# Who zeroes the third value buffer, and the order of turns, logits and divisions, in a fused attention and mixture-of-experts kernel

## The chip, the cores and the metric

The kernel runs on one core of a Trainium2 chip. The metric is the device time of one execution in microseconds (us). The kernel before takes 343.18 us, the median of three runs between 341.76 and 344.17. The engines are named as the profile names them: PE multiplies matrices and turns (transposes) tiles, DVE is the vector engine, ACT the scalar engine, POOL the GpSimd engine, which here also issues most loads, and SP issues the other transfers. Each engine works through its own list of instructions in order and waits where one needs a result that is not there yet.

## The reference

First an attention over chunks of 32 positions (4 batches, 8 heads, 768 positions, head dimension 64). Each chunk sees 16 positions before it, 8 behind it and 8 memory positions:

```python
scores = scale * np.matmul(q_c, k_full.transpose(0, 1, 3, 2))
scores = scores - np.max(scores, axis=-1, keepdims=True)
a = np.exp(scores)
a = a / (np.sum(a, axis=-1, keepdims=True) + 1e-09)
out[:, :, c_start:c_end] = np.matmul(a, v_full)
```

Its result, 3072 rows of 512, goes to a router with 8 experts. Each row takes the two experts with the highest noisy logits:

```python
logits = x @ w_gate
noise_scale = np.log1p(np.exp(x @ w_noise))
noisy_logits = logits + noise_scale * noise
top2 = np.argpartition(-noisy_logits, 2, axis=1)[:, :2]
...
h = np.maximum(x[mask] @ w1[e], 0.0)
out[mask] += top2_w[mask, k, None] * (h @ w2[e])
```

## The kernel before, in words

**Units.** The attention runs in 16 units, numbered i = 0 to 15 here. One unit is half of the positions of a group of four heads; there are eight groups, and a group has two units, an even one and the odd one behind it. A batch is four units. Queries and keys are loaded by group and must be turned before they can be used; one turn (`qkT_pe(n)`, line 243) handles a pair of heads, and a group has two pairs, so there is one turn per unit. The scores of both units of a group need both of its pairs.

**What one unit does.** On PE the probabilities of the unit before are turned (`PT_pe`, line 312), then queries and keys of a later pair (`qkT_pe`, line 250), then come the value products of the unit before (`PV_pe`, lines 326 and 330), the scores of the next unit (`scores_pe`, lines 275 to 290), and the turn of a finished output (`xT_pe`, line 354). DVE takes the maximum of the scores (line 298), copies the turned probabilities (line 317), subtracts the maximum (line 303), and divides the unit before by its sums (`mult_dve`, lines 342 and 343). ACT copies the turned queries (line 253), takes the exponential (line 305), copies the turned keys in two halves (`kT_act`, line 261) and copies the turned output (line 356). The order on each engine is the order in which the loop of line 576 calls these steps; it is written out by hand (`manual_schedule`), and no planner moves anything.

**Buffers.** Scores have one buffer (two PSUM banks), value products have one (three banks), and everything that is turned, the logits and the small products of the router share three (`psT`). A PE instruction that needs a buffer waits until its last reader is done. Turned queries and keys have four buffers each, so turns can run ahead: `ahead(i)` says which pairs unit i turns. Up to unit 4 that is pair i + 2, in unit 5 pairs 7 and 8, and from unit 6 on pair i + 3.

**Values.** Value tiles lie in three buffers, used by the eight groups in the order 0, 1, 0, 2, 1, 0, 2, 1. The places that no load writes must be zero, so each buffer is zeroed once before its first load: `clear_v` on ACT, `zero_v` (line 136) on DVE or POOL, and two direct fills on POOL (lines 570 and 571). A buffer has 24 chunks of 512 bf16 elements per partition; `zero_v` fills six of them. DVE's fills are issued as 32-bit words, POOL's as bf16. Buffer 1 has one fill on DVE in unit 0, and buffer 2 has three on DVE in units 2, 3 and 4 and one on POOL in unit 3. The loads themselves (lines 112 and 120) are issued by POOL.

**Routing inside the attention.** When four units of a batch b are finished, `begin_route(b)` computes the logits (line 365, PE), their exponential, logarithm and a copy (lines 380 to 384, ACT), and the noisy logits and their differences (lines 392 to 407, POOL for batches 0 to 2). It runs in units 6, 10 and 14. The rest follows in stages, one per unit: selection (lines 399 to 424 on DVE, the pair table of line 430 and its products, lines 472 and 473, on POOL), ranks (lines 437 to 442 on PE, 448 to 460 on DVE), comparison with a ramp (line 465, DVE) and the table of rows (line 480, PE; 486 or 488, DVE). `early_steps` runs the PE part of a stage ahead of the value products, `late_steps` the rest. The fourth batch is routed after the last unit, in one go, on DVE.

**The end.** Finished rows go to DRAM (`write_rows`, SP). After the fourth batch's table, POOL gathers rows per expert pair by indirect transfers (line 682) and the experts run: `first` (line 746) and `second` (line 754), with their weights loaded by POOL (lines 523 and 528).

These lines of the loop are the ones that move:

```python
            if fresh:
                begin_route((i - 3) // HP)
...
            if i < NPAIR - 1:
                late_steps()
            if i in (2, 3, 4):
                zero_v(2, i - 2)
            if i >= 1:
                mult_dve(i - 1)
```

Of the kernel before, what the change touches and what calls it, by code (L numbers as in the profile page):

```python
# [20 lines left out]
I32 = mybir.dt.int32  # L21
# [3 lines left out]
def kernel(  # L25
# [14 lines left out]
    nc = tc.nc  # L40
# [12 lines left out]
    HP = H // 2  # L53
# [31 lines left out]
    def body():  # L85
# [16 lines left out]
        def new_group(g):  # L102
            qg = ap_.tile([128, 2 * GP, SJ * D], BF16, name="qg", bufs=3)
            kg = ap_.tile([128, 2 * GP, SJ * D], BF16, name="kg", bufs=3)
            groups[g] = (qg, kg, vbufs[turn_of[g]])
# [25 lines left out]
        def zero_k(x):  # L131
            for hh in range(2):
                nc.vector.memset(kbufs[x][64 * hh:64 * hh + 64, 1 - hh, :], 0.0)

        def zero_v(x, j, eng=None):
            (eng or nc.vector).memset(vbufs[x][:, 6 * j:6 * j + 6], 0.0)  # L136

        new_group(0)
        load_qk(0, 0)
        identb = const.tile([128, 128], BF16, name="identb")  # L140
# [113 lines left out]
                else:  # L254
                    st[n]["p_k"] = p_t

        def kT_act(n):
            st[n]["kT"] = kbufs[n % NKB]
            for hh in range(2):
                hs = slice(64 * hh, 64 * hh + 64)  # L260
                nc.scalar.copy(st[n]["kT"][hs, hh, :].rearrange("d (p j) -> d p j", j=SJ), st[n]["p_k"][hs].rearrange("d j p -> d p j"))  # L261

# [38 lines left out]
        def sub_dve(n):  # L301
            sd = ap_.tile([128, 2, BT, CTX], F32, name="sd")
            nc.vector.tensor_tensor(out=sd, in0=st[n]["ps"], in1=bc4(st[n]["mx"], CTX), op=Alu.subtract)  # L303
            P = ap_.tile([128, 2 * UB, 4, QW], BF16, name="P")
            nc.scalar.activation(out=P.rearrange("p x h c -> p h x c"), in_=sd.rearrange("p x (h u) (e c) -> p (x h) (u e) c", h=2, e=2), func=Act.Exp, scale=scale)  # L305
            st[n]["P"] = P
# [8 lines left out]
        def PT_dve(n):  # L315
            PT = ap_.tile([128, 2 * UB, 128], BF16, name="PT")
            nc.vector.tensor_copy(PT, st[n]["p_p"])  # L317
            st[n]["PT"] = PT
# [219 lines left out]
        def begin_route(b):  # L538
            logits_pe(b)
            begin, *rest = route(b)  # L540
            begin()
            while pending:
                early_steps()
                late_steps()
            pending.extend(rest)
            for x in ((1,), (2, 3))[b] if b < 2 else ():
                load_noise(x)
# [19 lines left out]
        new_group(2)  # L567
        load_qk(2)
        memory_values(0, 2)
        nc.gpsimd.memset(vbufs[1][:, 12:15], 0.0)  # L570
        nc.gpsimd.memset(vbufs[1][:, 21:24], 0.0)
        def ahead(i):
            return [i + 2] if i < NEAR else [n for n in (i + 2, i + 3) if n < NPAIR and (i == NEAR or n > i + 2)]

        NEAR = 5
        for i in range(NPAIR):
            if i >= 1:
                PT_pe(i - 1)
            max_dve(i)
            for n in ahead(i):  # L580
                qkT_pe(n)
            fresh = i >= 3 and (i - 3) % HP == HP - 1
            if fresh:
                begin_route((i - 3) // HP)
            early_steps()
            if i >= 1:
                PT_dve(i - 1)
            sub_dve(i)
            if i == 0:
                zero_v(1, 1)  # L590
                load_v(1)
                new_group(3)
                load_qk(3)
            if i == 1:
                zero_k(3)
            for n in ahead(i):
                kT_act(n)
            if i >= 1:
                PV_pe(i - 1)
            if i + 1 < NPAIR:  # L600
                scores_pe(i + 1)
            if i < NPAIR - 1:
                late_steps()
            if i in (2, 3, 4):
                zero_v(2, i - 2)
            if i >= 1:
                mult_dve(i - 1)
                if i - 1 == NPAIR - 2:
                    write_rows(B, B - 1, 0, UB, 0, XC)
            if i >= 2:  # L610
                xT_pe(i - 2)
            if i == 2:
                load_v(2)
                memory_values(2, NG)
            for n in ahead(i):
                g = n // GP + 3
                if n % GP == 1 and g < NG:
                    new_group(g)
                    load_qk(g)
            if i == 3:  # L620
                zero_v(2, 3, nc.gpsimd)
                ramps()
                load_router()
            if i == 4:
                load_v(3)
            if i == 5:
                constants()
            if i >= 4 and i % GP == 0 and i // GP + 2 < NG:
                load_v(i // GP + 2)
            if i == GP * (NG - 3) + 1:  # L630
                load_w1(0)
                load_w2(0)
                load_w1(1)
        n = NPAIR - 1
        PT_pe(n)
        PT_dve(n)
        xT_pe(n - 1)
        late_steps()
        PV_pe(n)
        mult_dve(n)  # L640
        write_rows(B + 1, B - 1, UB, BT, 0, XC)
        early_steps()
        xT_pe(n)
        late_steps()
# [323 lines left out]
```

## Time and profile before

| what | value |
|---|---|
| runs | 341.76, 343.18, 344.17 us |
| profiled execution | 340.9 us, span 339.2 us |
| mean granted clock of PE over the span | 0.968 |
| PE busy | 295.1 us (87%) |
| DVE busy | 170.8 us (50%) |
| ACT busy | 132.5 us (39%) |
| POOL busy | 137.9 us (41%) |
| maximum of the first unit starts | at 14.6 us |
| maximum of the last unit starts | at 88.6 us |
| first expert product (line 746) starts | at 112.9 us |

The busy time of an engine is an average over stages with different limits: up to about 97 us the attention, then the last routing, then the experts. The share alone therefore does not say what sets the time. A row of the timeline gives start, length, engine, line, operation, what it writes and reads, the shapes, and in brackets the idle time of the engine before it and what ended that. A row of the chain gives start, length and what. Times count from the start of the span.

### The profile page before, as it was taken

To read this page: it belongs to the slowest core of one execution; us is meant where nothing else is said; L and a number is where in the kernel's file an instruction comes from. 1 tells how busy PE (TensorE), PEld (TensorE's weight loads), DVE (VectorE), ACT (ScalarE), POOL (GpSimd) and SP (SyncE) were. 2 spreads that over 40 slices of the span, in tenths; PEclk is the share of its full clock that TensorE was granted. 3 is DMA by queue.
4 is the path that set the end of the run, shared out by engine and by line. 5 is a ranking of instruction groups with operands and counts; after the bars stand their busy time and mean duration, and the time that the engine had idled before them with its cause. 6 is when DMAs were issued, how large, how long until landed. Compare 5 with 4: busy or idle time off the path is not lost.

```text
span 339.2 us, 8160 instructions
## 1 busy us (share of the span) xinstructions
PE 295.1 (87%) x3492; PEld 180.0 (53%) x3492; DVE 170.8 (50%) x341; ACT 132.5 (39%) x232; POOL 137.9 (41%) x181
## 2 busy tenths in 40 slices
PE   1687888898753859999999999999999999999990
PEld 1566676776542645548547545545545545545540
DVE  7788779889686653224224233224413424434430
ACT  7867888795430423343333323223123113103100
POOL 8878885392233686400062043034250132141161
PEclk9999999999985699999999999999999999999997
DMA  7999999999991379970059129518849227221031
GB/s 102 183 180 192 187 164 198 221 104 164 228 276 26 96 111 226 224 130 2 2 84 229 31 60 198 95 56 148 181 107 200 57 80 126 40 93 53 6 130 66
DMA packets 58407, 42.87 MB, mean 126 GB/s; under 512 B 32215, under 2 KB 51799, under 8 KB 58368
## 3 DMA queue, kind: packets, MB, share of 16 engines
q0 software_dynamic: 49808, 38.80, 68.9%
q1 hardware_dynamic: 8272, 3.44, 4.7%
q8 instruction: 29, 0.48, 0.5%
q10 hardware_dynamic: 288, 0.07, 0.1%
q14 instruction: 10, 0.08, 0.1%
HBM read 61.32 MB, written 10.65 MB: 212 GB/s over the span
## 4 chain that ended last, share of the span: by engine, by line
PE 54%; issue 16%; DVE 15%; ACT 6%; POOL 5%; DMA 1%; POOLq 0%; DVEq 0%
PE ps_h L746 23%; PE ps_y L754 19%; POOL out_dram L762 4%; ACT kd L261 3%; DVE vg L136 2%; DVE mx L298 2%; DVE sd L303 2%; PE p_t L691 2%; DVE xrow L343 2%; PE ps_o L330 2%; PE ps_o L326 2%; ACT xt L356 2%; ACT P L305 1%; ACT qT L253 1%; PE ps_s L285 1%
## 5 line engine op out<-in xcount | busy, mean ns | idle before, releaser
L746 PE MATMUL ps_h<-xTb,w1t 128*128 128x512 bf16 (+3 forms) x608 | 106.6, 325 | 2.0 <-DVE xTb L692 2.0
L754 PE MATMUL ps_y<-w2t,ht 128*128 128x512 bf16 x448 | 102.0, 379 | 0.0
L746 PEld LDWEIGHTS <-w1t 128*128 128x128 bf16 x864 | 64.1, 97 | 45.2 <-DVE xTb L692 1.6
L762 POOL DMA_INDIRECT out_dram<-acc,sidx x28 | 27.9, 995 | 139.2 <-DVE acc L761 135.0
L734 DVE TENSOR_SCALAR ht<-ps_h 128x416 bf16<-128x416 f32 (+2 forms) x64 | 39.9, 625 | 72.8 <-PE ps_h L746 72.8
L732 ACT ACTIVATE ht<-ps_h 128x416 bf16<-128x416 f32 (+2 forms) x72 | 37.9, 526 | 76.7 <-PE ps_h L746 72.4
L754 PEld LDWEIGHTS <-ht 128*128 128x128 bf16 x448 | 41.9, 98 | 46.6
L758 ACT ACTIVATE acc<-ps_y,meta 128x512 f32<-128x512 f32 x28 | 19.2, 687 | 69.3 <-PE ps_y L754 56.5
L746 PE MATMUL ps_h<-xTs,w1t 128*128 128x32 bf16 x256 | 45.4, 177 | 0.2 <-DVE xTs L707 0.2
L761 DVE SCALAR_TENSOR_TENSOR acc<-ps_y,meta,acc 128x512 f32<-128x512 f32 x28 | 21.0, 751 | 37.0 <-PE ps_y L754 37.0
L682 POOL DMA_INDIRECT xl<-x_rows,gidx x28 | 29.7, 1061 | 15.4 <-issue 6.1
L120 POOL DMA_DIRECT2D vg<-in_v_dram x34 | 25.3, 753 | 8.2 <-PE ps_s L290 3.4
L692 DVE COPY xTb<-p_t 128x512 bf16<-128x512 bf16 x28 | 11.7, 422 | 29.0 <-PE p_t L691 29.0
L261 ACT COPY kd<-p_t 64x768 bf16<-64x768 bf16 x32 | 25.2, 786 | 1.0 <-PE p_t L250 0.7
L250 PE MATMUL p_t<-identb,qg 128*64 128x128 bf16 x192 | 10.3, 245 | 8.2 <-DMA qg<-in_q_dram 6.3
L305 ACT ACTIVATE P<-sd 128x768 bf16<-128x768 f32 x16 | 13.5, 844 | 9.5 <-DVE sd L303 9.5
L356 ACT COPY xt<-p_x 128x768 bf16<-128x768 bf16 x16 | 12.8, 798 | 8.0 <-PE p_x L354 7.7
L343 DVE TENSOR_TENSOR xrow<-ps_o,rec 128x768 bf16<-128x768 f32 x16 | 15.3, 958 | 0.6
L326 PE MATMUL ps_o<-memv,PT 128*128 128x260 bf16 x96 | 13.7, 279 | 2.0 <-DVE PT L317 2.0
L298 DVE TENSOR_REDUCE mx<-ps_s 128x12 f32<-128x768 f32 x16 | 15.1, 941 | 0.6 <-PE ps_s L285 0.6
L303 DVE TENSOR_TENSOR sd<-ps_s,mx 128x768 f32<-128x768 f32 x16 | 15.2, 947 | 0.0
L253 ACT COPY qT<-p_t 128x768 bf16<-128x768 bf16 x16 | 12.8, 800 | 5.0 <-PE p_t L250 4.7
(146 smaller groups left out, 305.6 us busy)
## 6 DMA issues: line engine op xcount, KB each, us to landing
w1t<-in_moe_w_dram POOLq DMA_DIRECT2D x8, 1024.0 KB
w2t<-in_moe_w_dram POOLq DMA_DIRECT2D x8, 1024.0 KB
vg<-in_v_dram POOLq DMA_DIRECT2D x30, 168.0 KB
qg<-in_q_dram POOLq DMA_DIRECT2D x7, 384.0 KB
kg<-in_k_dram POOLq DMA_DIRECT2D x7, 384.0 KB
x_rows<-xrow SPq DMA_DIRECT2D x3, 792.0 KB
x_rows<-xrow SPq DMA_DIRECT2D x2, 384.0 KB
xl<-x_rows,gidx POOLq DMA_INDIRECT x28
```

Source lines behind the costliest of these rows:

```text
L120: nc.gpsimd.dma_start(out=vg[p0 + j:p0 + j + nj, c:c + n, hd, :, :].rearrange("p c e d -> p c (e d)"), in_=bass.AP(v.tensor, v.offset + (g ...
L261: nc.scalar.copy(st[n]["kT"][hs, hh, :].rearrange("d (p j) -> d p j", j=SJ), st[n]["p_k"][hs].rearrange("d j p -> d p j"))
L298: nc.vector.tensor_reduce(out=mx, in_=st[n]["ps"], axis=AX, op=Alu.max)
L303: nc.vector.tensor_tensor(out=sd, in0=st[n]["ps"], in1=bc4(st[n]["mx"], CTX), op=Alu.subtract)
L343: nc.vector.tensor_tensor(out=xr.rearrange("p u (h d) -> p u h d", d=D), in0=po[:, :, :MD].rearrange("p u (h d) -> p u h d", d=D), in1=rec ...
L682: nc.gpsimd.indirect_dma_start(out=xl, out_offset=None, in_=xd, in_offset=bass.IndirectOffsetOnAxis(ap=gidx[:, p:p + 1], axis=0), bounds_c ...
L732: nc.scalar.activation(out=dst, in_=src, func=Act.Relu)
L734: nc.vector.tensor_scalar(out=dst, in0=src, scalar1=0.0, scalar2=None, op0=Alu.max)
L746: nc.tensor.matmul(out=ps_h[:, o:o + w], lhsT=w1t[:, kp, f * 128:(f + 1) * 128], rhs=rhs(kp), start=(kp == 0 and i == 0), stop=(kp == KP - ...
L754: nc.tensor.matmul(out=ps_y, lhsT=ht[:, f, j * CAP:(j + 1) * CAP], rhs=w2t[:, f, :], start=(f == 0), stop=(f == FB - 1))
L761: nc.vector.scalar_tensor_tensor(out=a, in0=ps_y, scalar=gate, in1=a, op0=Alu.mult, op1=Alu.add)
L762: nc.gpsimd.indirect_dma_start(out=out_part[p], out_offset=bass.IndirectOffsetOnAxis(ap=sidx[:, p:p + 1], axis=0), in_=a, in_offset=None, ...
```

## The change

1. A new helper `wipe_v` zeroes a stretch of a value buffer on POOL, seen as 32-bit integers. It takes over the two fills of buffer 1 that POOL had as bf16, the fill of buffer 1 that DVE had in unit 0, and all of buffer 2: chunks 0 to 11 in unit 1 and 12 to 23 in unit 3. DVE keeps the fills of buffer 0 and one of buffer 1 before the loop.
2. `ahead(i)` is pair i + 2 in every unit that has one.
3. From unit 1 on, the first half of the turned keys is copied by ACT ahead of the unit's exponential, the second half behind it.
4. `begin_route` stands behind the scores of the next unit, ahead of the late steps; before, it stood behind the turn.
5. In the last unit the late steps (the selection of batch 2) stand behind the subtraction; before, they came after the loop. The division of unit 14 and the write of its rows move from the last unit to behind the copy of the last turned probabilities, and the turn of output 14 moves behind the last value products.

```diff
+        def wipe_v(x, lo, hi):
+            nc.gpsimd.memset(vbufs[x][:, lo:hi].bitcast(I32), 0)
...
-        def kT_act(n):
+        def kT_act(n, which=(0, 1)):
             st[n]["kT"] = kbufs[n % NKB]
-            for hh in range(2):
+            for hh in which:
...
-        nc.gpsimd.memset(vbufs[1][:, 12:15], 0.0)
-        nc.gpsimd.memset(vbufs[1][:, 21:24], 0.0)
+        wipe_v(1, 12, 15)
+        wipe_v(1, 21, 24)
+        wipe_v(1, 6, 12)
         def ahead(i):
-            return [i + 2] if i < NEAR else [n for n in (i + 2, i + 3) if n < NPAIR and (i == NEAR or n > i + 2)]
-
-        NEAR = 5
+            return [i + 2] if i + 2 < NPAIR else []
+
         for i in range(NPAIR):
...
             fresh = i >= 3 and (i - 3) % HP == HP - 1
-            if fresh:
-                begin_route((i - 3) // HP)
             early_steps()
             if i >= 1:
                 PT_dve(i - 1)
+            if i >= 1:
+                for n in ahead(i):
+                    kT_act(n, (0,))
             sub_dve(i)
             if i == 0:
-                zero_v(1, 1)
                 load_v(1)
...
+            if i == NPAIR - 1:
+                late_steps()
             for n in ahead(i):
-                kT_act(n)
+                kT_act(n, (1,) if i >= 1 else (0, 1))
             if i >= 1:
                 PV_pe(i - 1)
             if i + 1 < NPAIR:
                 scores_pe(i + 1)
+            if fresh:
+                begin_route((i - 3) // HP)
             if i < NPAIR - 1:
                 late_steps()
-            if i in (2, 3, 4):
-                zero_v(2, i - 2)
-            if i >= 1:
+            if 1 <= i < NPAIR - 1:
                 mult_dve(i - 1)
-                if i - 1 == NPAIR - 2:
-                    write_rows(B, B - 1, 0, UB, 0, XC)
             if i >= 2:
                 xT_pe(i - 2)
+            if i == 1:
+                wipe_v(2, 0, 12)
...
             if i == 3:
-                zero_v(2, 3, nc.gpsimd)
+                wipe_v(2, 12, 24)
...
         n = NPAIR - 1
         PT_pe(n)
         PT_dve(n)
-        xT_pe(n - 1)
-        late_steps()
+        mult_dve(n - 1)
+        write_rows(B, B - 1, 0, UB, 0, XC)
         PV_pe(n)
         mult_dve(n)
         write_rows(B + 1, B - 1, UB, BT, 0, XC)
+        xT_pe(n - 1)
         early_steps()
         xT_pe(n)
         late_steps()
```

## The prediction

> **What bounds the kernel now.** The profiled execution took 340.9 us, of which the span is 339.2 us; the median of the three runs shown is 343.18 us, 2.3 us more. I make the sum against the profiled execution and carry the difference over to the median unchanged.
>
> I read first the page's chain that ended last, its shares by line.
>
> ```profile
> PE ps_h L746 23%; PE ps_y L754 19%; POOL out_dram L762 4%; ACT kd L261 3%; DVE vg L136 2%; DVE mx L298 2%; DVE sd L303 2%; PE p_t L691 2%; DVE xrow L343 2%; PE ps_o L330 2%; PE ps_o L326 2%; ACT xt L356 2%; ACT P L305 1%; ACT qT L253 1%; PE ps_s L285 1%
> ```
>
> The expert stage (lines 746 and 754) holds 42% of the span, and the diff does not touch it: it can only start earlier or later. Everything else is decided in the sixteen attention units and in the routing behind the last of them, where the chain is passed between DVE, ACT and PE. The question is what one unit costs. Here is the chain through unit 13, which has no fill and no turn in it (start, length, what).
>
> ```profile
> 79.80 0.87 DVE mx L298
> 80.67 0.47 DVE PT L317
> 81.19 0.84 PE ps_o L326 x6
> 82.03 0.78 PE ps_o L330 x24
> ```
>
> Maximum, copy of the turned probabilities, then the value products end at 82.81, 3.0 us after the maximum began. On DVE the reciprocal and the division follow, and the next maximum is queued behind them.
>
> ```profile
> 34.74 0.95 DVE L303 TENSOR_TENSOR sd<-ps_s,mx 128x768 f32<-128x768 f32 x1
> 35.96 1.34 DVE L136 MEMSET vg<- 128x1536 uint32 x1 [0.27 <-issue]
> 37.21 0.17 DVE L342 RECIPROCAL rec<-ps_o 128x12 f32<-128x12 f32 x1
> 37.42 0.96 DVE L343 TENSOR_TENSOR xrow<-ps_o,rec 128x768 bf16<-128x768 f32 x1
> 38.29 0.95 DVE L298 TENSOR_REDUCE mx<-ps_s 128x12 f32<-128x768 f32 x1
> ...
> 43.19 0.23 DVE L342 RECIPROCAL rec<-ps_o 128x12 f32<-128x12 f32 x1 [2.63 <-PE ps_o L330]
> 43.46 0.96 DVE L343 TENSOR_TENSOR xrow<-ps_o,rec 128x768 bf16<-128x768 f32 x1
> 44.34 0.44 DVE L224 CAST ramp<-ramp_i 128x128 bf16<-128x128 int32 x1
> ```
>
> From reciprocal to the next DVE operation it is 44.34 - 43.19 = 1.15 us. So a unit cannot be shorter than 3.0 + 1.15 + about 0.1 of hand-over, **4.3 us**. Whatever DVE does between the subtraction and the end of the value products (some 0.9 us) is free; what goes beyond it is paid. The reader sees both in these rows. Unit 4's maximum began at 34.74 - 0.47 - 0.87 = 33.40, so it took 4.89 us with the fill of line 136 in it; unit 5 (38.29 to the maximum behind 44.34 and three small casts, 44.76) took 6.47, and its reciprocal waited 2.63 us for PE.
>
> Why PE was late is in PE's and ACT's own timelines.
>
> ```profile
> 32.83 0.25 PE L285 MATMUL ps_s<-kd,qT 128*32 128x80 bf16 x4 [1.18 <-ACT kd L261]
> ...
> 41.05 0.53 PE L250 MATMUL p_t<-identb,kg 128*64 128x128 bf16 x12 [0.89 <-ACT qT L253]
> ```
>
> ```profile
> 27.93 0.80 ACT L356 COPY xt<-p_x 128x768 bf16<-128x768 bf16 x1
> 29.27 0.80 ACT L253 COPY qT<-p_t 128x768 bf16<-128x768 bf16 x1 [0.54 <-PE p_t L250]
> 30.45 0.84 ACT L305 ACTIVATE P<-sd 128x768 bf16<-128x768 f32 x1 [0.39 <-DVE sd L303]
> 31.20 1.58 ACT L261 COPY kd<-p_t 64x768 bf16<-64x768 bf16 x2
> ```
>
> In an odd unit the scores of the next group need the key that the same unit turns (two ahead); unit 3's waited 1.18 us for it. Unit 5 turns two pairs, and the second one's key transposes waited 0.89 us for a buffer.
>
> **The change part by part.** *Fills.* Three fills of 1.34 us leave DVE in units 2 to 4 and one in unit 0. How much of each stood beyond the free 0.9 us: in unit 4 the reciprocal began at 37.21 where the value products, a quarter of a us late behind the turn, would have let it go at 33.40 + 3.4 = 36.8, so 0.4; in unit 2, whose turn is not late, about 0.55; in unit 3 nothing, since the key decides. In unit 0 no quoted row tells where the next scores end, so between nothing and 1.34; I take 0.35, near the other units. What DVE drops, POOL takes.
>
> ```profile
> L136 DVE MEMSET vg<- x8: 1338/1338/1338, 2.3 to 36.0; 128x1536 uint32 x8
> ...
> L570 POOL MEMSET vg<- x1: 1377/1377/1377, 14.7 to 14.7; 128x1536 bf16 x1
> L571 POOL MEMSET vg<- x1: 1377/1377/1377, 16.0 to 16.0; 128x1536 bf16 x1
> L136 POOL MEMSET vg<- x1: 2657/2657/2657, 34.7 to 34.7; 128x3072 bf16 x1
> ```
>
> POOL pays by the element: 1377 ns for 1536, 2657 for 3072. No row shows it filling many 4-byte words. If a word costs what a bf16 element costs, twelve chunks (3072 words) take 2.66 us, the two small fills fall to 0.74, and POOL has 2 x 2.66 + 1.38 + 2 x 0.74 - (2.66 + 2 x 1.38) = 2.8 us more. If time goes by bytes, it is 2.8 + 7.7 = 10.5 us. I take the first, since DVE's own 1536 words take 1338 ns, nearly POOL's time for as many elements. POOL issues the loads, but group 3's buffer is not read before unit 7, so I charge nothing; without that cover it would be up to the 2.8. The last query and key loads are issued a unit later too, behind a value load, and are read only in unit 12. The Trainium skill, VectorE: DVE Perf Modes, section Zero memsets can be issued as uint32 (trn2), states one cycle per element whatever the dtype; it speaks of VectorE, no run here shows it for POOL, and by it the sum would be the same 2.8 us.
>
> *Half of the key ahead of the exponential.* ACT's four operations, 0.80 + 0.80 + 1.58 + 0.84, are 4.0 us. In unit 3 it idled 0.54 and 0.39; the first half (0.79) goes where the 0.39 was, so the second half ends about 0.45 us earlier. The exponential slips by 0.4, hidden: its reader comes a unit later. With an even unit ahead, whose ACT is done early, I reckon 4.5 us for an odd unit (scores end, 0.5 to the copy, 3.6 of ACT, 0.5 of scores); unit 3 itself gains 0.5. Units 0 to 4 together: 0.35 + 0.55 + 0.5 + 0.4, **-1.8**.
>
> *One turn in unit 5.* 6.47 becomes 4.3 plus 0.42 of casts, which the key's 4.5 does not exceed: 4.75, **-1.7**. The price comes back in odd units, whose key is no longer a unit ahead: unit 13, 4.3 before, becomes 4.5, **+0.2**; unit 9 has the six comparisons of the ranks on DVE and units 7 and 11 the selection, which are as long by themselves.
>
> *Logits behind scores.* They stand ahead of the value products in units 6 and 10 (chain):
>
> ```profile
> 46.42 0.74 PE ps_l L365 x24
> ...
> 66.63 0.69 PE ps_l L365 x24
> ```
>
> Both leave the path: **-1.4**. What is late next: in units 7 and 11 the turn of the probabilities stands behind the logits on PE and ends some 1.1 us after the maximum began, by my count, where DVE would take it at 0.87: 0.2 us each, **+0.4**. The noise loads that the step issues on SP have nothing behind them that waits. And the batch's selection is late against its unit, on POOL:
>
> ```profile
> 70.69 3.62 POOL L120 DMA_DIRECT2D vg<-in_v_dram  x5 [0.28 <-issue]
> 74.32 0.52 POOL L430 TENSOR_TENSOR oh<-two 128x192 bf16<-128x192 bf16 x1
> ```
>
> ```profile
> 76.48 0.25 PE L437 MATMUL ps_r<-oh,upper 128*128 128x168 bf16 x1 [0.18 <-ACT qT L253]
> ```
>
> The pair table (line 430) is queued behind five load issues, 3.62 us, and ends at 74.84, 1.64 us before PE wants it in unit 12. The logits of batch one move behind 0.84 + 0.78 us of value products and some 0.8 of scores, less 0.4 by which these start earlier: 2.0 us later in their unit. Units 10 and 11 together are 0.5 us shorter. 2.5 against 1.64 and a hand-over: PE waits about **+1.0** at the head of its queue, with unit 12's value products and the next scores behind it.
>
> *The end.* DVE's last units:
>
> ```profile
> 92.46 0.23 DVE L342 RECIPROCAL rec<-ps_o 128x12 f32<-128x12 f32 x1 [0.88 <-PE ps_o L330]
> ...
> 94.07 0.19 DVE L399 TENSOR_REDUCE m<-nl 128x6 f32<-128x48 f32 x1
> ...
> 95.90 0.23 DVE L342 RECIPROCAL rec<-ps_o 128x12 f32<-128x12 f32 x1
> ```
>
> The selection of batch two (94.07 to 95.8, 1.73 us) lay in the shadow of the last value products. Moved ahead of unit 14's division it fills an idle 0.88 us and pushes the rest: the last value products need the one output buffer that this division frees. 1.73 - 0.88 = **+0.85**. SP's row writes move with the divisions, far ahead of the first gather.
>
> Sum: -1.8 - 1.7 - 1.4 + 0.2 + 0.4 + 1.0 + 0.85 = -2.45, **-2.5**. The profiled execution would take 338.4, the median 343.18 - 2.5 = **340.7**.
>
> **The rivals.** *One, faster:* the two new waits don't come, since POOL gets its load issued in time or the last products start anyway. For it: both are small differences of long queues. Against: the buffer and queue orders are fixed. -2.5 - 1.0 - 0.85 = -4.35: 338.8.
>
> *Two, slower:* the turn's wait comes back in full in odd units 5, 7, 9, 11 and 13. Place: PE's scores behind the key's second half. It decides where the turn's query copy ends after the subtraction; then the half put ahead only delays. For it: the 0.54 us that ACT waited for PE. Unit 3's maximum stands in the chain at
>
> ```profile
> 28.23 0.86 DVE mx L298
> ```
>
> so that unit took 33.40 - 28.23 = 5.2; less 4.3 it is 0.9 each, 4.5 for five, in place of the 0.6 already charged: -2.5 + 3.9 = +1.4, 344.6. Against: in unit 3 the query copy ended (29.27 + 0.80) before the subtraction let ACT go on.
>
> *Three:* the clock.
>
> ```profile
> 112.00:116.00 4.00, 3.48 (x19) 2.37 (x17) 3.55 (x5) 1.12 (x3) 3.29 (x3) 0.50 0.36 100
> 116.00:120.00 4.00, 2.73 (x35) 2.14 (x32) 2.91 (x13) 2.12 (x8) 2.16 (x3) 1.00 0.24 68
> ```
>
> The granted clock (third column from the end) is 0.50 as the experts begin and 1.00 from 116 us. If the return does not move with the stage, 2.5 us more run at half speed, +1.25: 341.9. The Trainium skill, TensorE: Matmul & The Clock Gate, section What's actually happening, has the clock granted by free-running windows of 3413 ns, by which the return could stay where it is; one profile cannot show whether it does.
>
> *Four, not what it says:* POOL's words go by bytes. The 7.7 us then stand ahead of the issues of groups 2 to 4, and no quoted row tells what these have in hand, so between nothing and 7.7; I take 3, near one such issue (3.62 us): +0.5, 343.7. For it: no row of POOL excludes it; against: DVE's rate.
>
> **How the numbers follow.** One per cent is about what a measurement of this kernel can tell from no change. Chances: my forecast 0.34, rival one 0.27, two 0.14, three 0.08, four 0.07, two of the last three together 0.10 (two and four 347.6). The range leaves out that last case and a little of the first: 338.2 (rival one with units 7 and 11 free too) to 345.0. Faster by over 1% (under 339.75): rival one and 0.03 of the forecast, 0.30; slower by over 1% (over 346.6): 0.10; within: 0.60.
>
> **What would show it.** Fills: no line 136 on DVE behind unit 0, POOL's at 0.74, 1.38 and 2.66. Turns: unit 5 near 4.75, PE's waits for the key under 0.8 in odd units. Logits: behind the scores in units 6 and 10, and a PE wait for the pair table in unit 12. End: unit 14's division right behind the selection, last value products waiting for it. I am wrong if odd units take over 5 us, if a load of values stops PE in units 5 to 9, or if the wait in unit 12 is missing.

## The result, and the profile after

The changed kernel takes **342.15 us** (median of 20 runs, 339.6 to 346.5), the kernel before 341.69 us (median of 20 runs, the three shown at first among them). The ratio after to before is **1.0002, 95% interval 0.9977 to 1.0027**: no change that can be measured. I had said 2.5 us less, 0.73%, which the interval excludes. The time itself lies inside the range that I gave (338.2 to 345.0); that is luck, as the account below shows. Ratios and fits here and below use the fast runs, those that nothing disturbed; the medians are of all runs. The profiled execution took 341.32 us, its span 339.6 us, 0.4 us more than the one before.

The sixteen maxima of DVE cut the attention into units, as in the prediction. The rows of the maximum's line, of the kernel before (first) and of the changed kernel (line numbers are 3 higher in the loop, 6 in the expert part):

```profile
L298 DVE TENSOR_REDUCE mx<-ps_s x16: 895/947/958, 14.6 to 88.6; 128x12 f32<-128x768 f32 x16
```

```profile
L301 DVE TENSOR_REDUCE mx<-ps_s x16: 895/948/959, 14.6 to 89.0; 128x12 f32<-128x768 f32 x16
```

Both begin at 14.6 us and their last maxima are 0.4 us apart (88.62 and 89.01). Between them lies this (unit lengths in us, each the difference of two starts of the timeline; e2, e8 and e10 are experiments below):

| unit | 0 | 1 | 2 | 3 | 4 | 5 | 6 | 7 | 8 | 9 | 10 | 11 | 12 | 13 | 14 | to index table |
|---|---|---|---|---|---|---|---|---|---|---|---|---|---|---|---|---|
| before | 3.41 | 5.21 | 4.89 | 5.26 | 4.89 | 6.47 | 5.08 | 4.97 | 4.75 | 4.47 | 5.96 | 4.98 | 4.75 | 4.30 | 4.60 | 18.04 |
| after | 3.07 | 5.44 | 4.39 | 5.16 | 4.56 | 4.84 | 4.57 | 5.55 | 6.09 | 4.68 | 5.60 | 5.55 | 5.71 | 4.66 | 4.51 | 18.60 |
| e2 | 3.07 | 6.16 | 4.30 | 4.60 | 4.57 | 4.78 | 4.38 | 5.13 | 5.36 | 4.65 | 5.89 | 5.83 | 5.44 | 4.66 | 4.51 | 18.02 |
| e8 | 3.07 | 6.10 | 4.31 | 5.32 | 4.57 | 4.68 | 4.49 | 5.39 | 6.08 | 4.66 | 5.19 | 5.14 | 5.25 | 4.84 | 4.52 | 19.27 |
| e10 | 3.07 | 5.21 | 4.31 | 4.60 | 4.57 | 4.78 | 5.49 | 4.98 | 4.87 | 4.70 | 6.65 | 4.99 | 5.16 | 4.66 | 4.66 | 17.34 |

The changed kernel is 3.2 us ahead when unit 7 begins and 0.1 us behind when unit 13 begins; the end costs 0.6 more. So in these two executions 3.2 us are gained up to unit 7 and given back in units 7 to 12. Where PE was late there, its own timeline says (changed kernel; in brackets the idle time ahead and what ended it):

```profile
24.24 0.53 PE L253 MATMUL p_t<-identb,kg 128*64 128x128 bf16 x12 [0.49 <-DMA kg<-in_k_dram]
28.60 0.38 PE L253 MATMUL p_t<-identb,qg 128*64 128x128 bf16 x7 [0.46 <-issue]
...
41.46 0.20 PE L288 MATMUL ps_s<-kd,qT 128*32 128x80 bf16 x1 [0.88 <-issue]
46.56 0.75 PE L368 MATMUL ps_l<-wgn,xt 128*128 128x16 bf16 x24 [0.36 <-ACT kd L264]
...
51.63 0.25 PE L288 MATMUL ps_s<-kd,qT 128*32 128x80 bf16 x4 [0.47 <-ACT kd L264]
53.11 0.33 PE L357 MATMUL p_x<-identb,xrow 128*128 128x128 bf16 x3 [0.67 <-issue]
...
66.09 0.49 PE L329 MATMUL ps_o<-memv,PT 128*128 128x260 bf16 x3 [0.24 <-issue]
...
72.08 0.85 PE L333 MATMUL ps_o<-vg,PT 128*32 128x256 bf16 x24 [0.61 <-DMA vg<-in_v_dram]
76.68 0.23 PE L440 MATMUL ps_r<-oh,upper 128*128 128x168 bf16 x1 [1.14 <-POOL oh L433]
...
95.30 0.84 PE L329 MATMUL ps_o<-memv,PT 128*128 128x260 bf16 x6 [1.78 <-DVE xrow L346]
```

Two of these I had forecast: the pair table in unit 12 (1.14 us) and the last value products behind unit 14's division (1.78 us). Three kinds I had not: loads that land late (unit 2's key, unit 11's value), logits and keys that delay each other at 46.56 and 51.63, and "issue", idle time with no releaser in the profile: PE stops in the middle of a run of equal instructions, for 0.24 to 0.88 us.

POOL's fills, as whole rows of the groups:

```profile
L139 POOL MEMSET vg<- 128x3072 int32 x2 | 5.4, 2678 | 0.0
...
L139 POOL MEMSET vg<- 128x768 int32 x2 | 1.4, 737 | 0.1
L139 POOL MEMSET vg<- 128x1536 int32 x1 | 1.4, 1377 | 0.0
```

A 32-bit word costs POOL what a bf16 element cost it before (1377 ns for 1536, 2657 for 3072).

### The profile page after: what moved, and what is told of

The parts are those of the page before. It is cut to its first block, busy times and chain, and to the rows that moved or that the text cites. A ratio compares the mean times of both kernels' runs of the same rounds, so it can differ in the third digit from the quotient of the medians.

```text
span 339.6 us, 8160 instructions
## 1 busy us (share of the span) xinstructions
PE 294.8 (87%) x3492; PEld 179.7 (53%) x3492; DVE 167.0 (49%) x337; ACT 132.1 (39%) x232; POOL 141.0 (42%) x183
## 4 chain that ended last, share of the span: by engine, by line
PE 70%; DMA 7%; ACT 7%; DVE 6%; POOL 4%; issue 4%; POOLq 0%; DVEq 0%; ACTq 0%
PE ps_h L752 31%; PE ps_y L760 26%; DMA kg<-in_k_dram 4%; ACT kd L264 2%; PE ps_o L329 2%; PE ps_o L333 2%; ACT xt L359 2%; DMA wgn_f<-in_moe_w_noise_dram 2%; PE p_t L697 2%; POOL out_dram L768 1%; PE ps_s L288 1%; PE p_x L357 1%; PE ps_s L779 1%; ACT P L308 1%; ACT qT L256 1%
```

## The experiments

Ratios are to the kernel before, timed on the same chip in the same session. The last column of the table compares at equal clock: each run lists the mean granted clock of PE, and a straight line through the runs of a session, with one slope for all its kernels, rises by 0.9 to 1.4 us for every 0.005 that the clock is lower. The column gives the distance from the kernel before along that line (with its 95% uncertainty). It is not a time: where a kernel itself lowers its clock, the column leaves that loss out.

| kernel | median, us | before, us | ratio, 95% interval | at equal clock, us |
|---|---|---|---|---|
| e1 logits back | 342.61 | 341.84 | 1.0007 (0.9979 to 1.0036) | +0.2 ± 0.7 |
| e2 end back | 341.03 | 341.84 | 0.9989 (0.9961 to 1.0018) | -0.5 ± 0.6 |
| e3 both back | 342.58 | 341.84 | 1.0036 (1.0005 to 1.0066) | +0.1 ± 0.7 |
| e4 logits only | 343.59 | 341.84 | 1.0046 (1.0006 to 1.0085) | +1.2 ± 0.7 |
| e5 pad | 341.80 | 341.36 | 1.0010 (0.9984 to 1.0036) | +0.4 ± 0.6 |
| e6 end only | 342.41 | 341.36 | 1.0023 (0.9996 to 1.0050) | +0.7 ± 0.6 |
| e7 fills, half key | 342.01 | 341.36 | 0.9996 (0.9965 to 1.0027) | -0.2 ± 0.6 |
| e8 pair table early | 340.96 | 341.36 | 0.9966 (0.9927 to 1.0005) | -1.3 ± 0.6 |
| e9 logits last | 343.77 | 344.10 | 0.9973 (0.9926 to 1.0019) | -2.0 ± 0.6 |
| e10 both back, pad | 342.10 | 344.10 | 0.9962 (0.9924 to 1.0000) | -1.7 ± 0.6 |
| e11 before, pad | 343.46 | 344.10 | 0.9989 (0.9951 to 1.0026) | -0.3 ± 0.6 |
| e12 e8 with pad | 344.37 | 345.11 | 1.0000 (0.9965 to 1.0034) | -0.9 ± 0.7 |

### Undoing the logits and the end (e1 to e4)

e1 is the changed kernel with

```diff
+            if fresh:
+                begin_route((i - 3) // HP)
             early_steps()
...
                 scores_pe(i + 1)
-            if fresh:
-                begin_route((i - 3) // HP)
```

> The changed kernel with the logits put back ahead of the value products in units 6, 10 and 14 (with their activations and noise loads); everything else of the change stays. Theory A (the early gain of about 3 us is real, and the later logits give it back by pushing the selection, its turn of the probabilities and the pair table late in units 7, 8, 11 and 12): units 6 and 10 grow by 0.7 each, units 7, 8, 11 and 12 together shrink by about 3.3, so unit 13's maximum starts near 77.9 instead of 79.84 and the run takes about 1.9 us less than the changed kernel. Rival B (what is lost in units 7 to 13 is PE stopping for its own instructions and for loads of values, whatever the order): only unit 12's wait of 1.14 goes and 1.4 comes back in units 6 and 10, so unit 13's maximum stays within 0.5 us of 79.84 and the time is the same.

Measured: units 6 and 10 grow by 0.84 and 2.06, units 7, 8, 11 and 12 shrink by 0.57, 1.19, 0.57 and 0.54, and units 13 and 14 grow by 1.64 and 1.21; unit 13's maximum starts at 79.51. The time is that of before. The rows for units 10 and 13 are not about logits:

```profile
65.11 0.66 PE L368 MATMUL ps_l<-wgn,xt 128*128 128x16 bf16 x20 [1.12 <-issue]
```

```profile
85.44 0.32 PE L288 MATMUL ps_s<-kd,qT 128*32 128x112 bf16 x9 [1.44 <-issue]
```

Behind each of these two stops the granted clock is 0.50 for 3.4 us (from 66.0 and from 86.5 us). So theory A is right for the four units that it named (2.9 of 3.3 us), and rival B is right for the time.

e2 puts the end back:

```diff
-            if i == NPAIR - 1:
-                late_steps()
...
-            if 1 <= i < NPAIR - 1:
+            if i >= 1:
                 mult_dve(i - 1)
+                if i - 1 == NPAIR - 2:
+                    write_rows(B, B - 1, 0, UB, 0, XC)
...
         PT_dve(n)
-        mult_dve(n - 1)
-        write_rows(B, B - 1, 0, UB, 0, XC)
+        xT_pe(n - 1)
+        late_steps()
         PV_pe(n)
         mult_dve(n)
         write_rows(B + 1, B - 1, UB, BT, 0, XC)
-        xT_pe(n - 1)
```

> The changed kernel with only the end as before (unit 14's division ahead of the last selection of batch two's old place, row write and transposes with it). Theory A: from unit 14's maximum to the index table 18.0 us, as before, instead of 18.60, so 0.6 us less (my prediction had 0.85 for it). Rival B (the end is set by the half clock and by PE's transposes, not by DVE's order): 18.6 as in the changed kernel, no difference.

Measured: 18.02 us from the last maximum to the index table, as theory A has it; the time falls from the ratio 1.0002 to 0.9989, the right size but within both intervals.

e3 makes both edits, of which this is the core:

```diff
+            if fresh:
+                begin_route((i - 3) // HP)
             early_steps()
...
-            if 1 <= i < NPAIR - 1:
+            if i >= 1:
                 mult_dve(i - 1)
```

> The fills on POOL, the turns two units ahead and the half key ahead of the exponential alone; logits and end as before. Theory A: the two gains add up, 1.9 + 0.6 = 2.5 us less than the changed kernel, about 339.5, and 2 us under the kernel before. Rival B: 0.6 us less than the changed kernel, about the kernel before.

Measured: 1.2 us *slower* than the kernel before; both theories miss. Unit 7 begins 2.3 us ahead, then PE stops for 1.27 us in unit 8 and for 1.77 us at the end, and the granted clock is 0.50 from 53.6 to 57.0 and from 91 to 98 us:

```profile
53.70 0.39 PE L357 MATMUL p_x<-identb,xrow 128*128 128x128 bf16 x2 [1.27 <-issue]
```

```profile
91.14 0.71 PE L315 MATMUL p_p<-identb,P 128*128 128x128 bf16 x5 [1.77 <-issue]
```

At equal clock nothing of the 1.2 us is left (+0.1 ± 0.7).

e4 makes the opposite edit in the kernel before, alone:

```diff
-            if fresh:
-                begin_route((i - 3) // HP)
             early_steps()
...
                 scores_pe(i + 1)
+            if fresh:
+                begin_route((i - 3) // HP)
```

> The kernel before with the logits behind the scores as its only edit. Theory A: units 6 and 10 shrink by 0.7 each, units 7, 8, 11 and 12 grow by about 3.3 together: 1.5 to 1.9 us slower than the kernel before. Rival B: 1.4 less and a pair table's wait of up to 0.5 more: 1 us faster. The forecast's terms for it (-1.4 +0.4 and a wait that here has 1.64 us in hand against about 2.0) give -0.6.

Measured: 1.6 us slower (+1.2 at equal clock), the size that theory A gave, though units 7 and 11 hardly grow (0.1 each). Unit 6 gains 0.8 and unit 10 0.3, and units 8 and 12 lose 0.8 and 1.4, each with PE waiting for its batch's pair table, which POOL had queued behind loads:

```profile
56.98 0.23 PE L437 MATMUL ps_r<-oh,upper 128*128 128x168 bf16 x1 [0.79 <-POOL oh L430]
```

```profile
78.51 0.23 PE L437 MATMUL ps_r<-oh,upper 128*128 128x168 bf16 x1 [1.62 <-POOL oh L430]
```

### What the stops are, and the parts by themselves (e5 to e8)

e5 adds to the changed kernel, ahead of the first turn, matmuls that nothing reads:

```diff
+        pad = psT.tile([64, 8], F32, name="pad", tag="tr")
+        for _ in range(64):
+            nc.tensor.matmul(out=pad, lhsT=zeros, rhs=zeros[:, :8], start=True, stop=True)
         qkT_pe(0)
```

> The changed kernel with 64 small matmuls of zeros (128 TensorE instructions with their weight loads) put ahead of everything, where TensorE waits 6.5 us for the first query in any case. Theory F (TensorE stops for the next piece of its own instructions, which the DMA queues bring in pieces of 16 KB; a stop hits where the count of instructions says, not what the code does there): the stops of the changed kernel (p_t at 28.6 us, ps_s of unit 5 at 41.5, p_x at 53.1, ps_o of unit 10 at 66.1) are gone from these places and stand 128 instructions, about 2.5 us, earlier in the code: turns of the probabilities or value products of units 5 and 7, the pair table's products or transposes of unit 9 or 10. The time then moves by up to 1 us either way. Rival (the stops belong to the operations, a queue or a buffer there): they stay where they are and the time is the same.

```profile
1.01 3.58 PE L565 MATMUL pad<-zeros 128*64 128x8 bf16 x64 [1.01 <-DVE zeros L149]
6.08 0.85 PE L253 MATMUL p_t<-identb,qg 128*64 128x128 bf16 x12 [1.50 <-DMA qg<-in_q_dram]
...
37.69 0.38 PE L315 MATMUL p_p<-identb,P 128*128 128x128 bf16 x4 [0.34 <-issue]
...
67.46 0.68 PE L368 MATMUL ps_l<-wgn,xt 128*128 128x16 bf16 x21 [0.72 <-issue]
```

Measured: all four stops of the changed kernel are gone from their operations (the scores at 41.67 now wait 0.84 us for the key, p_x at 51.81 for nothing), and two others are there; the time does not change. Theory F for the stops, no verdict on the time. The count says more. If the matmuls of a trace are laid in order against the program's list of PE instructions, weight loads counted, the attention's stops stand at these numbers in all fourteen kernels:

| instruction | stops there (us) |
|---|---|
| 693 to 695 | p_t: before 0.56, after 0.46, e4 0.89, e6 1.42, e7 0.15, e8 0.62 |
| 1203 | ps_s: after 0.88, e1 0.46, e3 0.76, e8 0.20, e9 0.32; ps_o: e7 0.82; p_p: e5 0.34, e12 0.22 |
| 1713 to 1715 | p_x: after 0.67, e3 1.27, e8 0.67, e9 0.87; ps_s: e7 1.30 |
| 2219 to 2223 | p_t: before 0.37, e4 0.70, e7 0.74; ps_o: after 0.24, e2 0.53, e11 0.25; ps_l: e1 1.12 |
| 2473 to 2481 | p_t: e4 0.17, e6 1.13; ps_l: e5 0.72, e12 0.93; ps_s: e10 1.40; ps_o: e11 0.46 |
| 3239 to 3243 | p_p: before 1.01, e1 0.46, e3 1.77, e6 1.34, e7 0.47, e8 0.50, e9 0.17; p_x: e4 0.71 |

(Two more: p_x at 1967 to 1969 in the kernel before 0.21, e4 0.41 and e7 0.41, and ps_s at 2989 in e1 1.44.) The numbers lie about 255 apart, or a multiple of that, whatever the operation. The queues of the changed kernel's page have the other half:

```profile
q0 software_dynamic: 49808, 38.80, 69.0%
q1 hardware_dynamic: 8272, 3.44, 4.7%
q8 instruction: 29, 0.48, 0.5%
```

Queue 8 brings 29 pieces of instructions, 0.48 MB / 29 = 16 KB each, and the kernel's list for PE has some 7700 instructions (a loop that this execution skips included), about 265 to a piece. With the pad's 128 instructions more, queue 8 brings 30 pieces (e5, e10, e11 and e12). In every kernel each of these stops ended 1.2 to 1.6 us after a piece had come in. So **PE waits there for its own instructions**, as far as a profile that names no releaser can show it. What makes the same place cost 0.15 us in one kernel and 1.42 in another stays open.

e6 is the edit of e2 the other way round, in the kernel before:

```diff
+            if i == NPAIR - 1:
+                late_steps()
...
-            if i >= 1:
+            if 1 <= i < NPAIR - 1:
                 mult_dve(i - 1)
...
         PT_dve(n)
-        xT_pe(n - 1)
-        late_steps()
+        mult_dve(n - 1)
+        write_rows(B, B - 1, 0, UB, 0, XC)
         PV_pe(n)
```

> The kernel before with the new end as its only edit (selection of batch two ahead of unit 14's division, that division and its row write behind the loop, unit 14's transposes behind unit 15's division). My prediction's term: +0.85, with the last value products waiting for unit 14's division; the changed kernel against the one with the old end gave 0.58 in the profiles. Rival (the clock, not DVE's order, sets the tail; it would have been a change of the clock): nothing, and from unit 15's maximum to the index table 18.0 us as before.

Measured: ratio 1.0023, 0.8 us; 18.96 us from the last maximum to the index table where the kernel before has 18.04, and the wait is the one forecast:

```profile
95.71 0.84 PE L326 MATMUL ps_o<-memv,PT 128*128 128x260 bf16 x6 [1.78 <-DVE xrow L343]
```

Not all of the 0.92 us is the edit's: the stop ahead of the copy of unit 14's turned probabilities is 1.34 us here and 1.01 in the kernel before, and that copy comes 0.33 us later after the last maximum. From the copy to the index table it is 17.1 us in the four kernels with the new end (the changed one, e1, e5, e6) and 16.5 in the kernel before, e2, e10 and e11. So the edit costs 0.6 us: the term of +0.85 had the right place and was 0.25 too high.

e7 is e3 with the turns of the kernel before:

```diff
-            return [i + 2] if i + 2 < NPAIR else []
+            return [i + 2] if i < NEAR else [n for n in (i + 2, i + 3) if n < NPAIR and (i == NEAR or n > i + 2)]
+
+        NEAR = 5
```

> Fills on POOL and half of the key ahead of the exponential, but the turns three units ahead from unit 5 on, and logits and end as before. Theory S (two units ahead leaves the odd units no slack, and each stop of TensorE or late load then goes straight into the time): the lead is about 1.2 us at unit 5, none of it is lost in units 7 to 14, and the time is 1.2 us less than the kernel before, about 340.6. Rival (the lead of the early units is lost on late loads whatever the turns): same time as the kernel before.

Measured: no difference. The lead at unit 5 is 0.7, not 1.2; and it is lost in units 5 to 10, where this execution has stops of 0.82, 1.30, 0.41 and 0.74 us, so theory S, by which three units of lead would have hidden them, is not borne out.

e8 is e2 with two value loads later:

```diff
             if i < NPAIR - 1:
                 late_steps()
+            if i in (7, 11):
+                load_v((i - 1) // GP + 2)
...
-            if i >= 4 and i % GP == 0 and i // GP + 2 < NG:
+            if i in (4, 8):
                 load_v(i // GP + 2)
```

> The changed kernel with the old end, and the value loads of groups five and seven issued a unit later, behind the pair table of units 7 and 11 on POOL. By the prediction's step for unit 12 the wait of 1.0 goes: TensorE's ps_r of unit 12 no longer waits for oh, 1.0 us less than the changed kernel with the old end (341.0), so about 340. Rival: unit 12 then waits for the value loads or for the key instead, no difference.

Measured: the wait goes. Unit 12 of e2 and of e8:

```profile
75.63 0.23 PE L440 MATMUL ps_r<-oh,upper 128*128 128x168 bf16 x1 [0.87 <-POOL oh L433]
```

```profile
75.69 0.25 PE L440 MATMUL ps_r<-oh,upper 128*128 128x168 bf16 x1 [0.27 <-ACT qT L256]
```

Unit 11 doesn't wait for its values either (e2 waited 0.89 us for them at 71.30) and takes 5.14 us instead of 5.83. The time is 0.34% below the kernel before, 1.3 us at equal clock. The profiled execution of e8 shows what keeps such a gain from the end. Its last stop (0.50 us at 89.36) is followed by this (granted clock: third column from the end):

```profile
90.00:92.00 2.00, 1.53 (x14) 0.86 (x18) 1.27 (x2) 0.69 (x1) 1.69 (x5) 0.66 1.19 184
92.00:94.00 2.00, 2.00 (x32) 1.46 (x25) 0.66 (x2) 0.15 (x1) 0.00 (x0) 0.50 1.22 196
94.00:96.00 2.00, 1.83 (x26) 1.24 (x28) 1.93 (x6) 1.66 (x3) 0.00 (x0) 0.99 1.17 214
```

Half speed for (0.34 + 0.50 + 0.01) x 2 / 0.5 = 3.4 us. The value products that fall into it took 1.36 and 1.46 us, the next ones 0.81 and 0.82: 1.2 us more. One such stretch lowers the mean clock of the run by 0.5 x 3.4 / 340 = 0.005, the step by which the runs' clocks differ, and that step goes with 0.9 to 1.4 us. The Trainium skill, TensorE: Matmul & The Clock Gate, section What's actually happening, has the clock granted by free-running windows of 3413 ns; the 3.4 us here agree.

The same is in e1, e3 and e9: every stretch at half clock inside the attention began during such a stop (0.50 to 1.77 us long) or within 1.3 us of its end. A stop alone is not enough: e6 (1.42, 1.13 and 1.34 us), e7 (1.30) and e10 (1.40) have stops as long and no half clock behind them.

### Logits later still, and pads (e9 to e12)

e9 is e8 with `begin_route` and the late steps that follow it behind `xT_pe` of the same unit:

```diff
-            if fresh:
-                begin_route((i - 3) // HP)
...
             if i >= 2:
                 xT_pe(i - 2)
+            if fresh:
+                begin_route((i - 3) // HP)
+                late_steps()
```

> e8 with the logits moved once more, behind the turns of the divided rows (p_x, copied by ACT to xt) of the same unit. Theory K (in units 7 and 11 the logits' 0.7 us on TensorE and their three ACT operations, 0.57 us, now stand ahead of the odd unit's chain xt, qT, kd, P, kd, which the scores wait for; that is what the term of -1.4 left out): xt is copied while the logits run, the odd units 7 and 11 shrink from 5.39 and 5.14 to 4.7, about 1.0 us less than e8 together. Rival (ACT's copies wait for the selection or loads there anyway): units 7 and 11 stay, same time as e8.

Measured: units 7 and 11 take 5.32 and 5.31 (e8 5.39 and 5.14). ACT's key is ready 0.3 us earlier in unit 7, and then DVE sets the end: it works through copy, subtraction, selection and division without a pause, and the selection's comparison (line 416, at 49.15) starts 0.34 us later in the unit than in e10, right behind POOL's differences (48.29 + 0.83 = 49.12), which wait for the logits. Theory K falls for the size; the rival is nearer. Unit 8 takes 7.09 us: a stop of 0.87 us at 52.46, and half clock from 52.8 on. The time is 2.0 us under the kernel before at equal clock, but e9's runs were granted less clock (0.961 on average, the kernel before 0.964), and the ratio's interval includes 1.

e10 is e3, e11 the kernel before and e12 e8, each with e5's pad:

```diff
+        for _ in range(64):
+            nc.tensor.matmul(out=pad, lhsT=zeros, rhs=zeros[:, :8], start=True, stop=True)
         qkT_pe(0)
```

> e3 (fills, two units ahead and half key; logits and end as before) with the 64 small matmuls of e5 ahead of it. Theory F (e3's lead of 2.3 us at unit 7 is lost to TensorE's stops for its own instructions at a place where they count, and to the half clock that follows them): the stops of 1.27 and 1.77 us at 53.7 and 91.1 us go elsewhere, and the time falls by 1 us or more from e3's ratio of 1.0036 to 0.999 or less. Rival (e3 is slow for its order of work): the ratio stays at 1.003 to 1.004.

Measured: ratio 0.9962 where e3 had 1.0036, and the intervals don't meet. Both of e3's stops are gone; one of 1.40 us has come in unit 10:

```profile
67.33 0.40 PE L288 MATMUL ps_s<-kd,qT 128*32 128x112 bf16 x16 [1.40 <-issue]
```

e3 and e10 ran on different chips, each with its own runs of the kernel before.

> The kernel before with the same 64 small matmuls ahead of it. Theory F: its stops (p_t 28.9, p_t 65.8, p_p 89.7 us) move 128 instructions earlier; with turns three units ahead most places have slack, so the time changes by less than 0.5 us, unless the 1.01 us at 89.7 goes (then 1 us less). Rival: the same stops at the same operations.

Measured: the stops move to ps_o, as theory F has it. The stop of 1.01 us at 89.7 is gone as well, and the way from the last maximum to the index table is 0.67 us shorter (17.37 for 18.04), where the theory gave 1 us; in the times it is 0.3 ± 0.6 us less at equal clock, so they don't show it.

> e8 (the change with the old end and the value loads of groups five and seven behind the pair tables) with the 64 small matmuls of e5 ahead. Theory F: e8's stops (p_t 29.3, p_x 53.4, p_p 89.4 us, with a half clock behind the last) go, those of e5 come (p_p of unit 4, hidden, and ps_l of unit 10, 0.7); about 1 us less than e8, so 2 us less than the kernel before, ratio 0.994. Rival (e10's gain over e3 was the chip or chance): the ratio of e8, 0.9966, or above.

Measured: ratio 1.0000. The stops came and went as theory F has it (p_p at 37.64, 0.22 us, and ps_l at 67.80, 0.93 us, in unit 11, which takes 6.20), the time did not follow (-0.9 ± 0.7 at equal clock, e8 -1.3 ± 0.6). So the pad moves the stops in every kernel, but only e3 with e10 suggests that the time follows, and e5 with the changed kernel, e11 with the kernel before and e12 with e8 do not.

No version could be shown to beat the kernel before: e8, e9 and e10 lie 0.3 to 0.4% below it with intervals that reach 1. At equal clock they and e12 are clear of it (0.9 to 2.0 us less), so their orders may be better in themselves; the time that would follow from it is not shown.

## Why the prediction was right or wrong

The forecast's terms beside what the two profiled executions show, up to the index table of the gather:

| step of the prediction | forecast | measured |
|---|---|---|
| fills and half key, units 0 to 4 | -1.8 | -1.04 |
| one turn in unit 5 | -1.7 | -1.63 |
| logits, units 6 and 10 | -1.4 | -0.87 |
| units 7 and 11 | +0.4 | +1.15 |
| units 8 and 9 | 0 | +1.55 |
| pair table, unit 12 | +1.0 | +0.96 |
| units 13 and 14 | +0.2 | +0.27 |
| the end | +0.85 | +0.56 |
| sum | -2.45 | +0.95 |

Behind the index table the changed execution was 0.5 us faster, so that 0.4 us remain in the span; its granted clock is 0.50 from 102.9 to 116.5 us, in the execution before from 98.9 to 116.0.

That the median fell into the range is luck: steps that came out near their size were cancelled by losses that had no term. Of the 0.60 for "within one per cent", 0.31 was the forecast itself and the rest rivals two to four, none of which was seen.

**Right:** unit 5, the wait for the pair table (1.14 us, and gone with its cause in e8), and the place of the end's loss (the wait of 1.78, here and in e6; it costs 0.6 and not 0.85). Rival four fell with POOL's 737, 1377 and 2678 ns. **No test of rival three:** the experts began 1.1 us later, not earlier; the clock came back at 116.5 us (0.94 from 116 to 120 us) and before at 116.0, so it moved by half of that.

**Right in size, not kept here: "units 0 to 4 together -1.8".** Unit 0 gave its 0.35 (3.07 for 3.41), and units 2 to 4 of e2 have 4.30, 4.60 and 4.57, 1.6 us less than before, against 1.45 forecast. What took part of it back stands in unit 1, and I had no term for it: the first value products run while PE is still slow. The kernel before (first) and e2:

```profile
19.77 1.14 PE L326 MATMUL ps_o<-memv,PT 128*128 128x260 bf16 x6
20.83 0.85 PE L330 MATMUL ps_o<-vg,PT 128*32 128x256 bf16 x24
```

```profile
19.76 1.48 PE L329 MATMUL ps_o<-memv,PT 128*128 128x260 bf16 x6
21.17 1.48 PE L333 MATMUL ps_o<-vg,PT 128*32 128x256 bf16 x24
```

In later units the same products take 0.84 and 0.85. The record of the granted clock begins, at full clock, at 20.4 us in the kernel before, at 20.9 in the changed one and at 22.6 in e2 (the views print 1.00 ahead of it, and the mean clock doesn't count that stretch), and unit 1 takes 5.21, 5.44 and 6.16. Over the fourteen executions the moment lies between 20.3 and 22.8 us. It is late in e4 too (22.0, unit 1 takes 5.55), whose order up to there is that of the kernel before; whether the change has a part in it, single executions can't tell. e10, with these three parts of the change and the full clock at 20.4, takes 21.76 us for units 0 to 4, before 23.66: -1.9, as forecast. The rest of what is missing is the stop at 28.60, 0.6 us of unit 3 (5.16, in e2 4.60). The wait of 0.49 us for unit 2's key costs 0.1 (4.39, in e2 without it 4.30).

**Wrong, first: no term for units 8 and 9, and for "both leave the path" none for what the logits then stand ahead of.** In units 6 and 10 the 1.4 is there where no stop is in the way (e8: 4.49 and 5.19, where e3 with the logits ahead has 5.48 and 5.61). The 0.2 each for units 7 and 11 is right too where nothing else falls into them: 5.13 and 5.14 (unit 7 in e2, e5 and e12, unit 11 in e8), where the kernel before, e1, e3 and e10, all with the logits ahead, take 4.97 to 4.99. In the changed kernel's execution they take 5.55. In unit 7 the logits stand 0.36 us behind ACT's copy of a key (46.56), and the copy of the probabilities waits 0.42 us for PE; in unit 11 the values land 0.61 us late. The step moved ACT's three operations too, which I had not followed: logits, exponential, logarithm and copy now stand ahead of the odd unit's keys. The changed kernel's chain through unit 7:

```profile
46.56 0.76 PE ps_l L368 x24
47.32 0.02 issue
47.34 0.22 ACT ns L383
47.56 0.02 issue
47.59 0.24 ACT ns L384
47.83 0.09 ACT lg L387
47.92 0.70 ACT xt L359
48.62 0.71 ACT qT L256
49.33 0.69 ACT kd L264
50.02 0.74 ACT P L308
50.77 0.02 issue
50.79 0.80 ACT kd L264
51.59 0.04 issue
51.63 0.21 PE ps_s L288 x2
```

That this order on ACT costs the time is argued from the chain and not shown: in e9 the key is ready 0.3 us earlier, and units 7 and 11 still take 5.3 us.

Unit 8 had no term. It takes 4.75 to 4.90 where no stop falls in it and the logits are ahead (before, e1, e10), 5.24 to 5.36 behind (e5, e12, e2), and 6.09 here with a stop of 0.67 on top. For unit 9 the prediction held that the rank comparisons "are as long by themselves"; they are not. With the turns of the kernel before and no stop it takes 4.30 (e6; 4.47 in the kernel before, behind a stop of 0.21) and 4.65 to 4.70 with the turns two ahead (e1, e2, e8, e10), since PE waits there for the key as in unit 13 (0.47 and 0.57 us here). So two turns of lead cost 0.35 us in each of the two units, where I had 0 and 0.2. Units 1, 3, 7 and 11 take over 5 us and a load of values stops PE, both named as signs of being wrong, the load in unit 11 and not in units 5 to 9. In the kernel before, the later logits by themselves cost 1.6 us (e4), where my terms gave -0.6: there the pair table is late in units 8 and 12.

**Wrong, second: what "issue" is.** I had it only in rows of DVE and POOL, 0.27 and 0.28 us, and added no term for PE's. The stops are 2.15 us in the kernel before and 2.25 in the changed one, so their sum explains no difference; but they fall on other operations whenever the order of PE's instructions changes, and how much of each is on the path changes with it: of those in the kernel before, the one in unit 3 costs nothing (5.26, in e11 without it 5.27) and the one at 89.7 costs 0.67 us (e11); in the changed kernel, units 3 and 8 are 0.6 and 0.7 to 0.9 us longer than where there is none (5.16 and 6.09; e2 4.60 and 5.36, e5 4.60 and 5.24).

**The rivals.** Rival one's condition is gone, since both new waits came. Rival two's 0.9 us each for five odd units did not come: PE's waits for the key are 0.47, 0.47 and 0.57 us in units 7, 9 and 13.

**The start of the sum:** the 343.18 us of the three runs was 1.5 us above the median of twenty, so even a right difference would have given a time too high.

What stays open: whether fills, half key and two turns by themselves gain anything at the end. The nine kernels that have them begin unit 7 with a lead of 2.3 to 3.6 us in their profiled executions; the ratios of e3 and e10, which have nothing else, lie on opposite sides of 1. That stretches at half clock follow stops was seen (e1, e3, e8, e9) but not made to happen on purpose, and e5, which has none of the changed kernel's four stops, is no faster: it has others, a wait of 1.19 us for the pair table, and the full clock at 22.4 us.

## What to carry to other kernels

Of a step that is moved, follow each engine that it uses to the next thing in that engine's queue: the logits were freed on PE and landed ahead of the keys on ACT and behind the loads on POOL. Before you count a gain early in a pipeline, look for what comes at a time of its own there, since it takes the gain: here the moment at which PE reaches its full clock (up to 1 us of unit 1), and a load that lands just ahead of its use (0.6 us of waiting in unit 11). In a stage made of short waits, changes below one per cent vanish in PE's stops and in stretches at half clock; compare unit by unit in several traces, and the times at equal clock.

## What the runs showed of the hardware

PE's instructions come in pieces of 16 KB, and where the end of a piece falls into a dense run of products, PE stopped for 0.15 to 1.77 us, at the same instruction count in all kernels and with very different lengths; 128 instructions put in front made it stop at other operations. A stop can be followed by 3.4 us at half clock (in e1, e3, e8 and e9, but not behind stops of 1.13 to 1.42 us in e6, e7 and e10). At the start PE is slow until 20.3 to 22.8 us, at another moment in each execution, and the value products that fall into it take 1.48 us in place of 0.85. Each 0.005 of mean clock goes with 0.9 to 1.4 us of this kernel's time. And POOL zeroes 32-bit words at the price of bf16 elements, so half as many elements are half the time (1377 against 2657 ns for the same bytes).
